# A dense layer with mish: the first two tiles of x as two loads, and the opening taken tile by tile

## The chip, the core and the metric

The kernel runs on one core of a Trainium2 chip. The metric is device time in microseconds (us) of one execution. A profile of one execution shows every engine: TensorE (PE, with its weight loads as PEld), VectorE (DVE), ScalarE (ACT), GpSimd (POOL), and SyncE (SP), which here only issues DMAs. ACT issues some DMAs too.

## The reference

```
B, S, D, F = 1, 2048, 512, 1792          # all bf16
h   = einsum("bsd,df->bsf", x, w1) + b1
sp  = log1p(exp(-abs(h))) + max(h, 0)    # softplus
act = h * tanh(sp)                       # mish
out = einsum("bsf,fd->bsd", act, w2)
```

## The kernel before

Rows of x are split into 16 tiles of 128 and, for the first product, into four blocks of 512 rows (`BLOCKS`). D is split into four parts of 128, called k, and F into 14 parts of 128, called f. The first product puts h transposed into PSUM: for each f and block, four matmuls over k, with a 128x128 piece of w1 as the stationary operand and 512 columns of the transposed x (`xT`) as the moving one. ACT reads the finished bank, adds b1 and applies mish (line 163). The second product takes a 128-row piece of that as the stationary operand and 512 columns of w2, 14 matmuls for a tile of the output; DVE copies the bank out (line 208) and SP stores it. TensorE's order is written out by hand: first product of a block, its four output tiles, the next block.

Only the opening, block 0, is unlike this. Its x tiles 2 and 3 come transposed by a DMA (`t_x23`), but tiles 0 and 1 are loaded as they are into `x_nat` by one DMA, in which partition p holds rows 2p and 2p + 1, so that "tile" j is every second row; `rows` (line 191) stores the output in the same way. TensorE transposes them against an identity matrix, half a tile at a time, in `transpose_x` (line 136), in four groups: tile 0's k 0, tile 1's k 0, k 1 of both, k 2 and k 3 of both. Each group has two PSUM banks, and DVE or ACT copies it to `xT` (line 155). `free[bank]` keeps who must be done before a bank is written again.

While these loads run, TensorE does seven filler matmuls on constants into bank 7 (`WARM`, line 105). `t_fill[n]` says that filler n is done. SP issues x, then k 1 of w1 for the first eight f (`OPEN`); it waits for the third filler, then issues the transposing load of x tiles 2 and 3, k 3, b1, the rest of w1, w2 and the other blocks of x. ACT issues k 0 and k 2 of w1 for the first eight f, at once. `load_part` (line 96) makes one such load and notes for each (k, f) which semaphore says that it has landed. SP's and ACT's loads go over two DMA queues, q1 and q10.

The opening's products are in `first` (line 239), called for a range of f, some of the four tiles and some k: k 0 of tile 0 for f 0 to 3, k 0 of tile 1 for f 0 to 3 (128 columns each), k 0 of both for f 4 to 7, k 1 and k 2 of both for f 0 to 7 (256 columns), k 0 to 2 of tiles 2 and 3 (256 columns), and k 3 of all four (512 columns), which ends each f and lets mish start. f uses bank f % 8. In `mm1_step` (line 168) TensorE waits, ahead of a product, for the bank (at the first product into it), for the piece of w1, and for the copy of x.

Of the kernel before, what the change touches and what calls it, by code (L numbers as in the profile page):

```python
# [4 lines left out]

P = 128
SQ = 32
WARM = (512,) * 5 + (256,) * 2
BLOCKS = (512, 512, 512, 512)


# [21 lines left out]
def bass_standalone__dense_activation_mish__prompt_kernel(  # L33
# [16 lines left out]
    x2, out2 = x[0], out[0]  # L50
# [3 lines left out]
    OPEN = 8  # L54
    N0 = BLOCKS[0] // P

    with ExitStack() as es:
        def sb(name, shape, t):
            return es.enter_context(nc.sbuf_tensor(name, shape, t))

        x_nat = sb("x_nat", [P, 2, D], BF)
        xT = sb("xT", [P, KT, S], BF)
# [6 lines left out]
        ident = sb("ident", [P, P], BF)  # L69
        a_sb = sb("a_sb", [P, FT, S], BF)  # L70
        o_sb = sb("o_sb", [P, S // P, D], BF)
        ps = es.enter_context(nc.psum_tensor("ps", [P, 8, 512], F32))

        def sem(name):
            return es.enter_context(nc.semaphore(name))

        sp = Stream(nc.sync, None)
        pe = Stream(nc.tensor, sem("c_pe"))
        dve = Stream(nc.vector, sem("c_dve"))
        act = Stream(nc.scalar, sem("c_act"))  # L80
        pool = Stream(nc.gpsimd, sem("c_pool"))

        def load(q, dst, src, name, transpose=False):
            s = sem(name)
            (q.eng.dma_start_transpose if transpose else q.eng.dma_start)(dst, src).then_inc(s, 16)
            return (s, 16)

        def load_w1(q, ks, a, b):
            return load(q, w1_sb[:, ks, a * P:b * P], w1v[:, ks, a * P:b * P], "s_w1_%d_%d" % (ks.start, a))
# [6 lines left out]
        def load_part(q, k0, k1, a, b):  # L96
            t = load_w1(q, slice(k0, k1), a, b)
            for f in range(a, b):
                for k in range(k0, k1):
                    t_w1[k, f] = t  # L100

        t_bz = dve.mark(nc.vector.memset(b1_nat[:, :], 0.0))  # L102
        c_w = nc.const_aps.tensor(1.0, [P, P], BF)
        c_m = nc.const_aps.tensor(1.0, [P, 512], BF)
        t_fill = [pe.mark(nc.tensor.matmul(ps[:, 7, 0:n], c_w, c_m[:, 0:n], start=True, stop=True)) for n in WARM]  # L105

        act.eng.preload_act_table(ACT.Mish)  # L107
        act.wait(t_bz)
        for k in (0, 2):
            load_part(act, k, k + 1, 0, OPEN)  # L110
        t_xn = load(sp, x_nat[:, :, :], x2[0:2 * P, :].rearrange("(p j) d -> p j d", p=P), "s_xn")
        load_part(sp, 1, 2, 0, OPEN)
        sp.wait(t_fill[2])
        t_x23 = load(sp, xT[:, :, 2 * P:4 * P], x2[2 * P:4 * P, :], "s_x23", True)
        load_part(sp, 3, 4, 0, OPEN)
# [3 lines left out]
        t = load(sp, w2_sb[:, :, :], w2v, "s_w2")  # L119
# [3 lines left out]
        for s in range(1, len(BLOCKS)):  # L123
            lo, hi = starts[s], starts[s + 1]
# [5 lines left out]
        t_id = dve.mark(nc.vector.tensor_scalar(ident[:, :], diff[:, :], 0, None, ALU.is_equal))  # L130

        free = [[] for _ in range(8)]
        t_cp = {(j, k): t_x23 for j in (2, 3) for k in range(KT)}
        t_mish = {}

        def transpose_x():

            pe.wait(t_xn, t_id)
            H = P // 2
            for b0, eng, js, ks in ((0, dve, (0,), (0,)), (2, act, (1,), (0,)), (4, dve, (0, 1), (1,)), (6, act, (0, 1), (2, 3))):  # L140
                m = len(js)
                for i, k in enumerate(ks):
                    for n, j in enumerate(js):
                        lo = (i * m + n) * H
                        for h in (0, 1):
                            g = slice(h * H, (h + 1) * H)
                            mm = nc.tensor.matmul(ps[:, b0 + h, lo:lo + H], x_nat[g, j, k * P:(k + 1) * P], ident[g, g],  # L147
                                                  start=True, stop=True)
                eng.wait(pe.mark(mm))
                for i, k in enumerate(ks):  # L150
                    dst = xT[:, k, js[0] * P:(js[-1] + 1) * P].rearrange("p (j h t) -> p j h t", j=m, h=2)
                    src = ps[:, b0:b0 + 2, i * m * H:(i + 1) * m * H].rearrange("p h (j t) -> p j h t", j=m)
                    if m == 1:
                        dst, src = dst[:, 0], src[:, 0]
                    t = eng.mark(nc.vector.tensor_copy(dst, src) if eng is dve else act.eng.activation(dst, src, ACT.Copy))  # L155
                    for j in js:
                        t_cp[j, k] = t
                free[b0] = free[b0 + 1] = [t]

        def mish(s, f, bank, t_mm):  # L160
            n = BLOCKS[s]
            act.wait(t_b1c, t_mm)
            t = act.mark(act.eng.activation(a_sb[:, f, starts[s]:starts[s + 1]], ps[:, bank, 0:n], ACT.Mish,  # L163
                                            bias=b1_sb[:, f:f + 1]))
            t_mish[s, f] = t
            free[bank] = [t]

        def mm1_step(s, f, k, bank, js=None):

            n = BLOCKS[s]  # L170
            lo, hi = (0, n) if js is None else (js[0] * P, (js[-1] + 1) * P)
            first = k == 0 and lo == 0
            if first:
                pe.wait(*free[bank])
            pe.wait(t_w1[k, f])
            if s:
                pe.wait(t_xT[s])
            else:
                pe.wait(*[t_cp[j, k] for j in (js or range(N0))])
            return nc.tensor.matmul(ps[:, bank, lo:hi], w1_sb[:, k, f * P:(f + 1) * P],  # L180
                                    xT[:, k, starts[s] + lo:starts[s] + hi], start=first, stop=(k == KT - 1 and hi == n))
# [8 lines left out]

        def rows(i):

            if i < 2:
                return out2[0:2 * P, :].rearrange("(p j) d -> p j d", p=P)[:, i, :]
            return out2[i * P:(i + 1) * P, :]

        def mm2_step(i, f, lo, hi, bank):
# [7 lines left out]
        def put(i, lo, hi, bank, t_mm, q=sp):  # L205
            nonlocal n_out
            dve.wait(t_mm)
            t = dve.mark(nc.vector.tensor_copy(o_sb[:, i, lo:hi], ps[:, bank, 0:hi - lo]))  # L208
            free[bank] = [t]
            q.wait(t)  # L210
            q.eng.dma_start(rows(i)[:, lo:hi], o_sb[:, i, lo:hi]).then_inc(s_out, 16)
            n_out += 1
# [8 lines left out]
        def mm2_last(i):  # L221

            nonlocal n_out
            cuts = (0, D - 3 * P // 2, D - P // 2, D)
            toks = []
            for n, eng in enumerate((dve, dve, act)):
                lo, hi, bank = cuts[n], cuts[n + 1], 4 + (i + n) % 4
                for f in range(FT):
                    mm = mm2_step(i, f, lo, hi, bank)
                eng.wait(pe.mark(mm))  # L230
                dst, src = o_sb[:, i, lo:hi], ps[:, bank, 0:hi - lo]
                t = eng.mark(nc.vector.tensor_copy(dst, src) if eng is dve else act.eng.activation(dst, src, ACT.Copy))  # L232
                toks.append((lo, hi, t))
            for q, (lo, hi, t) in zip((sp, sp, act), toks):
                q.wait(t)
                q.eng.dma_start(rows(i)[:, lo:hi], o_sb[:, i, lo:hi]).then_inc(s_out, 16)
                n_out += 1

        def first(fs, js, ks, last=False):
            for k in ks:  # L240
                for f in fs:
                    mm = mm1_step(0, f, k, f % 8, js)
                    if last and k == KT - 1:
                        mish(0, f, f % 8, pe.mark(mm))


        def spread_b1():
            dve.wait(t_b1)
            for j in range(P // SQ):
                t = dve.mark(nc.vector.transpose(b1_T[j * SQ:(j + 1) * SQ, :], b1_nat[:, j * SQ:(j + 1) * SQ]))  # L250
            dve.wait(t)
            return dve.mark(nc.vector.tensor_copy(b1_sb[:, :], b1_T[:, 0:FT]))  # L252

        transpose_x()
        t_b1c = spread_b1()
        first(range(4), (0,), (0,))
        first(range(4), (1,), (0,))
        first(range(4, OPEN), (0, 1), (0,))
        first(range(OPEN), (0, 1), (1, 2))
        first(range(OPEN), (2, 3), (0, 1, 2))  # L260
        first(range(OPEN), None, (3,), True)
        for f in range(OPEN, FT):
# [41 lines left out]
```

## Time and profile before

| | |
|---|---|
| device time, three runs | 104.59, 105.42, 107.27 us (median 105.42) |
| span of the profiled execution | 102.9 us |
| device time of the profiled execution itself | not given; the median lies 2.5 us above the span |
| TensorE busy | 100.2 us, 97% of the span |
| DVE, ACT busy | 13.1 us, 39.5 us |
| fillers (line 105) | 7, from 0.77 us |
| transposes (line 147) | 16, from 3.43 us |
| first product | 4.13 us |

The span runs from the first to the last instruction; the device time has the start and end of the execution around it. Busy shares are averages. For a change in the first microseconds, the rows to read are the chain of work that ended last, the timeline of the opening, and the DMA issues with their times to landing. The chain follows the last instruction back to whatever released it. In a row of the timeline stand start, duration, engine, line, operation and output<-input; "x2" says that two instructions are merged.

### The profile page before, as it was taken

What the parts mean: (1) busy time and instruction counts of PE and PEld (TensorE: products, weight loads), DVE (VectorE), ACT (ScalarE), POOL (GpSimd) and SP (SyncE); (2) the same over time, 40 slices, a digit from 0 to 9 for tenths busy, and PEclk for the clock granted to TensorE, in tenths of its full rate; (3) what the DMA queues carried; (4) which work ended last, traced back from release to release, by engine and by line L of the source; (5) the groups of instructions that cost most, each with busy time, mean ns of one, the idle gap of its engine ahead of it and who ended that gap; (6) DMA issues with size and microseconds to landing.
All of it is one profiled execution on the core that took longest, in us unless ns stands there. A gap on an engine that the chain in (4) does not pass through costs nothing.

```text
span 102.9 us, 1196 instructions
## 1 busy us (share of the span) xinstructions
PE 100.2 (97%) x527; PEld 48.8 (47%) x527; DVE 13.1 (13%) x26; ACT 39.5 (38%) x61; POOL 0.4 (0%) x5
## 2 busy tenths in 40 slices
PE   6999999999999999999999999999999999999993
PEld 2697444444444444444444444444444444444472
DVE  1203000220220000022220000022201000020241
ACT  4301999000047777000017777400006777700000
POOL 1000000000000000000000000000000000000000
DMA  2999999991110000011001000001111000001112
GB/s 61 375 283 358 363 243 112 269 237 51 51 51 0 0 6 0 0 51 51 20 31 51 0 0 10 0 3 48 51 51 51 0 0 0 0 6 51 51 51 51
DMA packets 12977, 7.94 MB, mean 77 GB/s; under 512 B 7980, under 2 KB 12332, under 8 KB 12972
## 3 DMA queue, kind: packets, MB, share of 16 engines
q1 hardware_dynamic: 12540, 7.33, 27.4%
q10 hardware_dynamic: 432, 0.54, 1.5%
q8 instruction: 4, 0.07, 0.3%
q14 instruction: 1, 0.01, 0.0%
HBM read 3.94 MB, written 2.10 MB: 59 GB/s over the span
## 4 chain that ended last, share of the span: by engine, by line
PE 97%; DVE 0%; ACT 0%; issue 0%
PE ps L180 47%; PE ps L202 47%; PE ps L105 3%; DVE xT L155 0%; ACT o_sb L232 0%; PE ps L147 0%
## 5 line engine op out<-in xcount | busy, mean ns | idle before, releaser
L163 ACT ACTIVATE a_sb<-ps,b_sb 128x512 bf16<-128x512 f32 x56 | 37.1, 698 | 47.9 <-PE ps L180 47.9
L180 PE MATMUL ps<-xT,w_sb 128*128 128x512 bf16 (+2 forms) x252 | 49.1, 355 | 0.2 <-DVE xT L155 0.2
L202 PE MATMUL ps<-w_sb,a_sb 128*128 128x512 bf16 (+3 forms) x252 | 49.1, 355 | 0.0
L180 PEld LDWEIGHTS ps<-xT,w_sb 128*128 128x128 bf16 x252 | 24.2, 98 | 24.1 <-DVE xT L155 0.3
L202 PEld LDWEIGHTS ps<-w_sb,a_sb 128*128 128x128 bf16 x252 | 23.2, 98 | 25.5
L208 DVE CAST o_sb<-ps 128x512 bf16<-128x512 f32 x15 | 10.4, 692 | 79.8 <-PE ps L202 79.8
L232 ACT ACTIVATE o_sb<-ps 128x64 bf16<-128x64 f32 x1 | 0.2, 224 | 11.5 <-PE ps L202 11.5
L105 PE MATMUL ps<-const-bfloat16-1.0 128*128 128x512 bf16 (+1 forms) x7 | 2.7, 566 | 0.8 <-PEq L289 0.8
L105 PEld LDWEIGHTS ps<-const-bfloat16-1.0 128*128 128x128 bf16 x7 | 0.9, 138 | 2.1 <-issue 2.1
L155 ACT ACTIVATE xT<-ps 128x256 bf16<-128x256 f32 (+1 forms) x3 | 0.9, 347 | 1.7 <-PE ps L147 1.7
L107 ACT ACT_TABLE_LOAD x1 | 1.3, 1283 | 0.7 <-PEq L289 0.7
L250 DVE STREAM_TRANSPOSE b_T<-b_nat 32x32 bf16<-32x32 bf16 x4 | 0.8, 202 | 3.3 <-DMA b_nat<-in_b_dram 3.2
L232 DVE CAST o_sb<-ps 128x320 bf16<-128x320 f32 (+1 forms) x2 | 0.8, 392 | 1.5 <-PE ps L202 1.5
L155 DVE CAST xT<-ps 128x128 bf16<-128x128 f32 (+1 forms) x2 | 0.6, 354 | 2.4 <-PE ps L147 2.4
L147 PEld LDWEIGHTS ps<-ident,x_nat 64*128 64x128 bf16 x16 | 0.4, 118 | 0.4 <-DMA x_nat<-in_x_dram 0.4
L147 PE MATMUL ps<-ident,x_nat 64*128 64x64 bf16 x16 | 0.5, 222 | 0.0
L130 DVE TENSOR_SCALAR ident<-diff 128x128 bf16<-128x128 int32 x1 | 0.2, 227 | 0.2 <-POOL diff L128 0.2
L128 POOL IOTA diff<- 128x128 int32 x1 | 0.2, 234 | 0.4 <-POOLq L289 0.4
L102 DVE MEMSET b_nat<- 32x64 uint32 x1 | 0.1, 112 | 0.8 <-PEq L289 0.8
L252 DVE CAST b_sb<-b_T 128x14 f32<-128x14 bf16 x1 | 0.2, 176 | 0.0
L289 POOL MEMSET const-bfloat16-1.0<- 128x1 bf16 x1 | 0.1, 102 | 0.0
L289 POOL MEMSET const-uint8-127<- 128x1 uint8 x1 | 0.1, 102 | 0.0
(2 smaller groups left out, 0.2 us busy)
## 6 DMA issues: line engine op xcount, KB each, us to landing
out_dram<-o_sb SPq DMA_DIRECT2D x15, 128.0 KB, 1.7
w_sb<-in_w_dram SPq DMA_DIRECT2D x1, 1792.0 KB, 10.7
w_sb<-in_w_dram SPq DMA_DIRECT2D x1, 768.0 KB, 6.1
w_sb<-in_w_dram ACTq DMA_DIRECT2D x2, 256.0 KB, 3.7
w_sb<-in_w_dram SPq DMA_DIRECT2D x2, 256.0 KB, 3.7
x_nat<-in_x_dram SPq DMA_DIRECT2D x1, 256.0 KB, 2.6
out_dram<-o_sb SPq DMA_DIRECT2D x1, 80.0 KB, 1.6
xT<-in_x_dram SPq DMA_TRANSPOSE x4, 5.0
```

The source lines that it names most:

```text
L105: t_fill = [pe.mark(nc.tensor.matmul(ps[:, 7, 0:n], c_w, c_m[:, 0:n], start=True, stop=True)) for n in WARM]
L107: act.eng.preload_act_table(ACT.Mish)
L128: t_diff = pool.mark(pool.eng.iota(diff[:, :], pattern=[[1, P]], base=0, channel_multiplier=-1))
L130: t_id = dve.mark(nc.vector.tensor_scalar(ident[:, :], diff[:, :], 0, None, ALU.is_equal))
L147: mm = nc.tensor.matmul(ps[:, b0 + h, lo:lo + H], x_nat[g, j, k * P:(k + 1) * P], ident[g, g], start=True, stop=True)
L155: t = eng.mark(nc.vector.tensor_copy(dst, src) if eng is dve else act.eng.activation(dst, src, ACT.Copy))
L163: t = act.mark(act.eng.activation(a_sb[:, f, starts[s]:starts[s + 1]], ps[:, bank, 0:n], ACT.Mish, bias=b1_sb[:, f:f + 1]))
L180: return nc.tensor.matmul(ps[:, bank, lo:hi], w1_sb[:, k, f * P:(f + 1) * P], xT[:, k, starts[s] + lo:starts[s] + hi], start=first, stop=( ...
L202: return nc.tensor.matmul(ps[:, bank, 0:hi - lo], a_sb[:, f, i * P:(i + 1) * P], w2_sb[:, f, lo:hi], start=(f == 0), stop=(f == FT - 1))
L208: t = dve.mark(nc.vector.tensor_copy(o_sb[:, i, lo:hi], ps[:, bank, 0:hi - lo]))
L232: t = eng.mark(nc.vector.tensor_copy(dst, src) if eng is dve else act.eng.activation(dst, src, ACT.Copy))
L250: t = dve.mark(nc.vector.transpose(b1_T[j * SQ:(j + 1) * SQ, :], b1_nat[:, j * SQ:(j + 1) * SQ]))
```

## The change

x tiles 0 and 1 are loaded by two DMAs, each of 128 consecutive rows, and the output of these tiles is stored in consecutive rows too. There are six fillers instead of seven. ACT waits for the second filler before it issues anything, and then issues k 0 of w1 as two loads (f 0 to 3, f 4 to 7; `HALF` is 4) and k 2. The transposes are done tile by tile: for each tile DVE copies k 0 and ACT copies k 1, 2 and 3 together, 128x384. The products then take k 0 of tile 0, k 0 of tile 1 and k 1 of both for f 0 to 3, k 0 and k 1 of both for f 4 to 7, and k 2 of both for f 0 to 7; the rest is as before.

```diff
--- before.py
+++ after.py
@@ -5,7 +5,8 @@
 
 P = 128
 SQ = 32
-WARM = (512,) * 5 + (256,) * 2
+WARM = (512,) * 5 + (256,)
+HALF = 4
 BLOCKS = (512, 512, 512, 512)
 
 
@@ -105,11 +106,12 @@
         t_fill = [pe.mark(nc.tensor.matmul(ps[:, 7, 0:n], c_w, c_m[:, 0:n], start=True, stop=True)) for n in WARM]
 
         act.eng.preload_act_table(ACT.Mish)
-        act.wait(t_bz)
-        for k in (0, 2):
-            load_part(act, k, k + 1, 0, OPEN)
-        t_xn = load(sp, x_nat[:, :, :], x2[0:2 * P, :].rearrange("(p j) d -> p j d", p=P), "s_xn")
+        t_xn = [load(sp, x_nat[:, i, :], x2[i * P:(i + 1) * P, :], "s_xn%d" % i) for i in range(2)]
         load_part(sp, 1, 2, 0, OPEN)
+        act.wait(t_fill[1])
+        load_part(act, 0, 1, 0, HALF)
+        load_part(act, 0, 1, HALF, OPEN)
+        load_part(act, 2, 3, 0, OPEN)
         sp.wait(t_fill[2])
         t_x23 = load(sp, xT[:, :, 2 * P:4 * P], x2[2 * P:4 * P, :], "s_x23", True)
         load_part(sp, 3, 4, 0, OPEN)
@@ -135,27 +137,26 @@
 
         def transpose_x():
 
-            pe.wait(t_xn, t_id)
             H = P // 2
-            for b0, eng, js, ks in ((0, dve, (0,), (0,)), (2, act, (1,), (0,)), (4, dve, (0, 1), (1,)), (6, act, (0, 1), (2, 3))):
-                m = len(js)
-                for i, k in enumerate(ks):
-                    for n, j in enumerate(js):
-                        lo = (i * m + n) * H
+            pe.wait(t_id)
+            for i in (0, 1):
+                pe.wait(t_xn[i])
+                for eng, b0, ks in ((dve, 2 * i, (0,)), (act, 4 + 2 * i, (1, 2, 3))):
+                    m = len(ks)
+                    for n, k in enumerate(ks):
                         for h in (0, 1):
                             g = slice(h * H, (h + 1) * H)
-                            mm = nc.tensor.matmul(ps[:, b0 + h, lo:lo + H], x_nat[g, j, k * P:(k + 1) * P], ident[g, g],
-                                                  start=True, stop=True)
-                eng.wait(pe.mark(mm))
-                for i, k in enumerate(ks):
-                    dst = xT[:, k, js[0] * P:(js[-1] + 1) * P].rearrange("p (j h t) -> p j h t", j=m, h=2)
-                    src = ps[:, b0:b0 + 2, i * m * H:(i + 1) * m * H].rearrange("p h (j t) -> p j h t", j=m)
+                            mm = nc.tensor.matmul(ps[:, b0 + h, n * H:(n + 1) * H], x_nat[g, i, k * P:(k + 1) * P],
+                                                  ident[g, g], start=True, stop=True)
+                    eng.wait(pe.mark(mm))
+                    dst = xT[:, ks[0]:ks[-1] + 1, i * P:(i + 1) * P].rearrange("p k (h t) -> p k h t", h=2)
+                    src = ps[:, b0:b0 + 2, 0:m * H].rearrange("p h (k t) -> p k h t", k=m)
                     if m == 1:
                         dst, src = dst[:, 0], src[:, 0]
                     t = eng.mark(nc.vector.tensor_copy(dst, src) if eng is dve else act.eng.activation(dst, src, ACT.Copy))
-                    for j in js:
-                        t_cp[j, k] = t
-                free[b0] = free[b0 + 1] = [t]
+                    for k in ks:
+                        t_cp[i, k] = t
+                    free[b0] = free[b0 + 1] = [t]
 
         def mish(s, f, bank, t_mm):
             n = BLOCKS[s]
@@ -190,8 +191,6 @@
 
         def rows(i):
 
-            if i < 2:
-                return out2[0:2 * P, :].rearrange("(p j) d -> p j d", p=P)[:, i, :]
             return out2[i * P:(i + 1) * P, :]
 
         def mm2_step(i, f, lo, hi, bank):
@@ -253,10 +252,11 @@
 
         transpose_x()
         t_b1c = spread_b1()
-        first(range(4), (0,), (0,))
-        first(range(4), (1,), (0,))
-        first(range(4, OPEN), (0, 1), (0,))
-        first(range(OPEN), (0, 1), (1, 2))
+        first(range(HALF), (0,), (0,))
+        first(range(HALF), (1,), (0,))
+        first(range(HALF), (0, 1), (1,))
+        first(range(HALF, OPEN), (0, 1), (0, 1))
+        first(range(OPEN), (0, 1), (2,))
         first(range(OPEN), (2, 3), (0, 1, 2))
         first(range(OPEN), None, (3,), True)
         for f in range(OPEN, FT):
```

## The prediction

> **What bounds the kernel now.** I read the page's totals first, then the chain of work that ended last in order of time.
>
> ```profile
> span 102.9 us, 1196 instructions
> ...
> PE 100.2 (97%) x527; PEld 48.8 (47%) x527; DVE 13.1 (13%) x26; ACT 39.5 (38%) x61; POOL 0.4 (0%) x5
> ```
> ```profile
> 0.77 2.72 PE ps L105 x7
> 3.49 0.19 PE ps L147 x3
> ...
> 3.70 0.30 DVE xT L155
> 4.00 0.12 issue
> 4.13 12.32 PE ps L180 x84
> 16.45 12.09 PE ps L202 x56
> ```
>
> TensorE is busy for 97% of the span, and from 4.13 us on nothing else is in the chain until the very end. The second and later stages are 56 matmuls of 512 columns in 12.09 us, 0.216 us each, so 256 columns take 0.108 and 128 columns 0.054. The change touches no product after the opening. So it can be worth only what it does to the time at which TensorE gets through the opening, and all of that lies in the first 4.13 us and in the waits that an earlier or later start meets behind them. The profiled execution has a span of 102.9 us; its own device time is not given. The median of the runs shown, 105.42, lies 2.5 us above the span, and I carry a difference in the span over to it one to one.
>
> Next the DMA, because the opening is fed by it: who issued what when, and how long each load took to land. The rows come from the timeline of SP and ACT and from the lists of DMA issues of short windows, where a load stands alone.
>
> ```profile
> 0.74 0.40 SPq L85 DMA_DIRECT2D x_nat<-in_x_dram  x1
> 0.95 0.86 ACTq L85 DMA_DIRECT2D w_sb<-in_w_dram  x2
> 1.19 0.42 SPq L85 DMA_DIRECT2D w_sb<-in_w_dram  x1
> 1.36 0.46 ACTq L85 DMA_DIRECT2D w_sb<-in_w_dram  x1
> 2.24 1.31 SPq L85 DMA_TRANSPOSE xT<-in_x_dram  x1
> 4.73 0.41 SPq L85 DMA_DIRECT2D w_sb<-in_w_dram  x1
> ```
> ```profile
> x_nat<-in_x_dram SPq DMA_DIRECT2D x1, 256.0 KB, 2.6
> w_sb<-in_w_dram ACTq DMA_DIRECT2D x1, 256.0 KB, 3.0
> w_sb<-in_w_dram SPq DMA_DIRECT2D x1, 256.0 KB, 3.6
> w_sb<-in_w_dram ACTq DMA_DIRECT2D x1, 256.0 KB, 4.3
> xT<-in_x_dram SPq DMA_TRANSPOSE x1, 4.4
> w_sb<-in_w_dram SPq DMA_DIRECT2D x1, 768.0 KB, 6.1
> ```
>
> Issue plus time to landing gives: x tiles 0 and 1 at 3.34, w1 k0 (first eight f) at 3.95, k1 at 4.79, k2 at 5.66, x tiles 2 and 3 at 6.64, the rest of w1 at 10.83. Against them stand the first uses, counted with the matmul times above: k1 at 4.13 + 8 x 0.054 + 4 x 0.108 = 4.99, k2 0.86 later at 5.86, x tiles 2 and 3 another 0.86 later at 6.72, the rest of w1 at 6.72 + 24 x 0.108 + 8 x 0.216 = 11.04. The slacks are 0.20, 0.20, **0.08** and 0.21 us. TensorE shows no wait, but each load arrives just ahead of its use.
>
> The last view is the DMA itself: the queues in the windows 1.78 to 2.78 and 2.78 to 3.44, then the busy share and rate by stretch (the last two columns).
>
> ```profile
> q1 hardware_dynamic: 116, 0.24, 94.6%
> ...
> q10 hardware_dynamic: 116, 0.24, 96.3%
> q1 hardware_dynamic: 26, 0.02, 9.3%
> ```
> ```profile
> 2.80:3.40 0.60, 0.60 (x3) 0.15 (x1) 0.00 (x0) 0.00 (x0) 0.00 (x0) 1.00 1.05 389
> 3.40:4.10 0.70, 0.56 (x17) 0.42 (x17) 0.40 (x2) 0.34 (x2) 0.00 (x0) 1.00 1.05 389
> 4.10:4.80 0.70, 0.67 (x11) 0.66 (x12) 0.23 (x1) 0.56 (x2) 0.00 (x0) 1.00 1.02 379
> ```
>
> q1 is SP's queue, q10 ACT's. The DMA engines are full, and they serve the loads **one after another**: in the first window only x moves, in the second almost only w1 k0, though k1 was issued on the other queue at 1.19. At 389 GB/s a load of 256 KB takes 0.67 us, half of one 0.34. So the landings of k1, k2 and x tiles 2 and 3 are set by the bytes ahead of them.
>
> **The change part by part.** *The filler.* One 256-column filler less. The first two rows below are weight loads, each made as a filler begins: the fifth at 2.43, the sixth at 2.86, one pitch of 512 columns (0.43 us) later. The sixth, of 256, streams for 0.21, so TensorE is free at 3.07 instead of 3.28, worth 0.21 if x is there.
>
> ```profile
> 2.43 0.15 PEld L105 LDWEIGHTS ps<-const-bfloat16-1.0 128*128 128x128 bf16 x1 [0.28 <-issue]
> 2.86 0.15 PEld L105 LDWEIGHTS ps<-const-bfloat16-1.0 128*128 128x128 bf16 x1 [0.28 <-issue]
> ...
> 3.42 0.42 PEld L147 LDWEIGHTS ps<-ident,x_nat 64*128 64x128 bf16 x16 [0.41 <-DMA x_nat<-in_x_dram]
> ```
> ```profile
> out_dram<-o_sb SPq DMA_DIRECT2D x15, 128.0 KB, 1.7
> ```
>
> *x as two loads.* The transposes now start at 3.42, 0.08 after x landed. No row shows a 128 KB load at this place; the 128 KB stores land 1.7 us after issue, so tile 0 lands between 2.44 and 3.34. I take 2.9, the middle, which leaves the filler's end, 3.07, as the start. Tile 1 finishes with the same 256 KB moved and lands at 3.34 as now. It costs SP one more issue, 0.45 us (0.74 to 1.19), so w1 k1 leaves SP at 1.64 instead of 1.19. The transpose load behind it waits for the third filler until 2.24 anyway, and k1 is off the queue by 2.06, so nothing later on SP moves. The stores of rows 0 to 255 only change their addresses.
>
> *Transposes and copies.* Still 16 transposes, now eight behind each tile. Copies by shape:
>
> ```profile
> L155 ACT ACTIVATE xT<-ps 128x256 bf16<-128x256 f32 x2 | 0.7, 381 | 0.0
> ...
> L155 DVE CAST xT<-ps 128x256 bf16<-128x256 f32 x1 | 0.4, 415 | 0.0
> L155 DVE CAST xT<-ps 128x128 bf16<-128x128 f32 x1 | 0.3, 292 | 2.4 <-PE ps L147 2.4
> ...
> L155 ACT ACTIVATE xT<-ps 128x128 bf16<-128x128 f32 x1 | 0.3, 278 | 1.7 <-PE ps L147 1.7
> ```
> ```profile
> L163 ACT ACTIVATE a_sb<-ps,b_sb 128x512 bf16<-128x512 f32 x56 | 37.1, 698 | 47.9 <-PE ps L180 47.9
> ```
>
> DVE gets two copies of 128x128 (2 x 0.292 for 0.292 + 0.415 now). ACT gets two of 128x384, a shape not in the trace: between 0.381 and 0.698, and 0.278 + 2 x 0.103 = 0.48 by the step from 128 to 256 columns, which I take. Now, transposes to first copy's end is 3.42 to 4.00, 0.58; so tile 0's k 0 is ready at 3.65 and tile 1's at 4.00. ACT starts tile 0 at about 3.50 (0.43 for the four transposes' pairs and their drain, 3.07 on) and ends it at 3.98, and ends tile 1 at 4.46. That copy carries k 1, so no k 1 product starts before about 4.50. And f 2 and 3 use the PSUM banks of tile 1's DVE copy: they wait until 4.0.
>
> *w1 k 0 behind the second filler, as two loads.* SP's transpose load leaves at 2.24 behind filler 3, so ACT's first half leaves one pitch earlier, at 1.81, instead of 0.95. Queued behind this wait on ACT are the second half (2.2) and k 2 (2.7 instead of 1.36), and the copies at 3.5, which are not delayed. Now k0 is second in the row of loads; behind the change x tile 0, x tile 1 and **k1 (1.64) have all been issued before it**. If loads are served in the order of issue, as all those of this trace were, the first half follows k1: 3.34 + 0.67 + 0.34 = 4.35. With the 0.08 from landing to TensorE the first product starts at 4.43 instead of 4.13. Bounds: if the half goes ahead of k1, 3.34 + 0.34 = 3.68, and the copies gate instead; if k1 takes the 0.84 that lay between the landings of k0 and k1 (3.95, 4.79) and the half as much as half of that, 4.60, a start at 4.68.
>
> The Trainium skill has a rule that speaks against the order of issue. In "DMA: Bandwidth & Descriptors", section "Queues, rings and completion order", it says that each DMA engine takes turns between the queues that have work, a packet at a time. By that rule the half would follow x tile 1, and k1 come third; the trace cannot decide, since its four loads alternate SP, ACT, SP, ACT.
>
> *The sum.* Start 4.43; j 0 and j 1 of f 0 to 3 take 8 x 0.054 (4.86); k1's copies are there (4.50), and the same 20 products of 256 columns as now lead up to x tiles 2 and 3 at 4.86 + 2.16 = 7.02, against 6.72 now. Those landed at 6.64; even the slip of some bytes stays covered, as do the rest of w1 (11.34 against 10.83) and k2 (6.16 against 5.66, with 0.5 to spare). So the slip of 0.30 goes through to the end: 105.42 + 0.30 = **105.7**. The filler's 0.21 and tile 0's earlier landing are not seen, since the weights are late. Forecast's own range by the bounds above: 105.6 to 106.0.
>
> **Rivals.** *The half of k0 goes ahead of k1 (not slower).* Then f 0 and 1 start at about 3.75, f 2 and 3 at 4.1, the 128-column products end at 4.43, k1 waits for ACT's copy to 4.50, and x tiles 2 and 3 are wanted at 6.66. They land at 6.64 and are usable at 6.72, where they are used now. Start 0.38 earlier, gain 0.00 to 0.06: 105.36 to 105.42. Even with x tiles 2 and 3 early, the rest of w1 allows no more than its slack of 0.21, 105.2. For it: the separate queue; against it: k1 is issued 0.17 earlier.
>
> *k2 falls behind x tiles 2 and 3.* k2 is now issued at 2.7, the transpose load at 2.24, as before. If the order turns, k2 lands where the transpose load did, 6.64, usable at 6.72, 0.86 later than now; if they share, half of it. Every product behind it slips: 105.42 + 0.43 to 0.86, about 106.1. It decides as soon as k2 lands past its first use, 5.8 to 6.2. Against it: the transpose load's issue takes 1.31 us, to 3.55, so its work may come late enough.
>
> *TensorE's clock.* Fillers come 0.43 apart for 512 columns, products 0.216: between 3.07 and 4.13 TensorE doubled its speed, 2.3 to 3.4 us after the first filler, though the page shows a granted clock of 1.00 throughout. With less filler and a hole from about 3.6 to 4.43, the step might need as long again from 4.43, at half speed: half of 2.3 to 3.4, 1.2 to 1.7 slower, 106.6 to 107.1. The fillers and transposes still cover nearly the same stretch, which speaks against it. "TensorE: Matmul & The Clock Gate" of the Trainium skill, Part 1, puts the step at a free-running window's end, whatever the kernel; by that, the phase would differ from run to run, before and after alike.
>
> **How the numbers follow.** Forecast 0.50, not slower 0.28, k2 late 0.15, clock 0.05, anything else 0.02. The cases run from 105.2 to 106.3, the clock aside. The three runs shown lie between 104.59 and 107.27, so a median of such runs can itself move by some tenths, and I widen by 0.6 below and 0.4 above: 104.6 to 106.7. Two per cent, about what a measurement of this kernel can tell from no change, is 2.1 us; only a clock that stays low through a run comes near it. Faster 0.01, within 0.95, slower 0.04.
>
> **What would show it.** In the profile after: the transposes from about 3.07 and in two groups; k0's first half landing near 4.35 with k1 ahead of it in the DMA windows; the first product at about 4.43 with a wait for w1 named ahead of it; the rest of the opening 0.3 later. A first product near 3.75 and a hole before k1 means the first rival, a wait ahead of k2's products the second, products 0.43 apart per 512 columns past 4.5 the third. I am wrong if the half lands before 3.8, or if x tiles 2 and 3 land so much earlier that an early start lasts.

## The result: 108.0 us, slower by 2.9%

The changed kernel takes 108.03 us (median of six runs, 107.64 to 111.77); the kernel before, run beside it, 105.12 (104.59 to 107.27). The ratio is 1.0294, 95% interval [1.0248, 1.0340]. The forecast was 105.7, its range 104.6 to 106.7. Ratios here and below leave out runs that lie over 1.5% above the fastest of their own kernel; for three kernels below (k2_on_sp, x23_plain, alternate) that is half of the runs or more, so for those the median of all runs stands beside the ratio.

The profiled execution of after has a span of 107.5 us, 4.6 more than before's. That is more than the 2.9 between the medians: in every run on record the device time lies 1.3 to 1.4 us above the span, so before's profiled execution (span 102.9) took about 104.2, as little as the fastest of its runs, while after's took 108.86, 0.8 above its median. Of the 2.5 us that the prediction saw between before's span and median, 1.2 are this, and its slacks are those of an execution in which things went well. What follows accounts for the 4.6 of this pair.

The page's totals, then the chain of work that ended last (start, duration, what):

```profile
span 107.5 us, 1187 instructions
...
PE 101.4 (94%) x517; PEld 49.5 (46%) x526; DVE 13.0 (12%) x26; ACT 39.5 (37%) x60; POOL 0.4 (0%) x5
```
```profile
2.23 0.46 ACTq L86
...
2.72 7.76 DMA w_sb<-in_w_dram
...
10.53 3.67 PE ps L181 x32
...
21.10 3.88 PE ps L201 x18
```

TensorE is busy for 101.4 us instead of 100.2, and idle for 6 instead of 3. In before nothing but TensorE's work stood in the chain from 4.13 us on. Here one load of w1, k 2, issued by ACT at 2.72, holds the end until 10.48. The second product of block 0 starts at 21.10 instead of 16.45: the 4.65 us are all lost before that, and nothing is added behind.

Who issued what and when, in SP's and ACT's timeline (start, duration, instruction, count):

```profile
0.74 0.87 SPq L86 DMA_DIRECT2D x_nat<-in_x_dram  x2
1.66 0.42 SPq L86 DMA_DIRECT2D w_sb<-in_w_dram  x1
2.25 1.31 SPq L86 DMA_TRANSPOSE xT<-in_x_dram  x1
...
1.82 1.35 ACTq L86 DMA_DIRECT2D w_sb<-in_w_dram  x3
```

And how long each took to land, from the lists of DMA issues of short windows around each issue (KB, us from issue to landing), in the order of issue: x tile 0, x tile 1, k 1, the two halves of k 0, x tiles 2 and 3, k 2.

```profile
x_nat<-in_x_dram SPq DMA_DIRECT2D x1, 128.0 KB, 2.1
x_nat<-in_x_dram SPq DMA_DIRECT2D x1, 128.0 KB, 2.0
w_sb<-in_w_dram SPq DMA_DIRECT2D x1, 256.0 KB, 3.7
w_sb<-in_w_dram ACTq DMA_DIRECT2D x1, 128.0 KB, 3.7
w_sb<-in_w_dram ACTq DMA_DIRECT2D x1, 128.0 KB, 4.3
xT<-in_x_dram SPq DMA_TRANSPOSE x1, 8.5
w_sb<-in_w_dram ACTq DMA_DIRECT2D x1, 256.0 KB, 7.8
```

x lands early, at 2.8 and 3.2. Then k 1 lands at 5.4 (before: 4.79), the halves of k 0 at 5.5 and 6.5 (k 0 before: 3.95), k 2 at 10.5 (before: 5.66) and x tiles 2 and 3 at 10.7 (before: 6.64). The bytes are the same. By stretch (last two columns: DMA busy share, GB/s), first after, then before:

```profile
5.40:6.40 1.00, 0.74 (x8) 0.77 (x9) 0.00 (x0) 0.00 (x0) 0.00 (x0) 1.00 1.23 94
6.40:7.40 1.00, 1.00 (x8) 0.73 (x7) 0.00 (x0) 0.00 (x0) 0.00 (x0) 1.00 1.15 128
...
8.40:9.60 1.20, 0.83 (x4) 0.28 (x2) 0.00 (x0) 0.00 (x0) 0.00 (x0) 1.00 0.99 152
```
```profile
5.40:6.40 1.00, 1.00 (x11) 0.90 (x10) 0.00 (x0) 0.00 (x0) 0.00 (x0) 1.00 1.19 296
6.40:7.40 1.00, 1.00 (x11) 0.90 (x10) 0.00 (x0) 0.00 (x0) 0.00 (x0) 1.00 1.05 269
...
8.40:9.60 1.20, 1.20 (x13) 0.98 (x11) 0.18 (x2) 0.00 (x0) 0.00 (x0) 1.00 1.01 361
```

Between 5.4 and 9.6 us the DMA engines count as fully busy, 0.99 to 1.23, in both kernels, but after moves 94 to 152 GB/s and before 269 to 361. So packets are under way and do not get done. The queues in the microsecond from 5.4, after and then before (packets, MB, share):

```profile
q10 hardware_dynamic: 21, 0.04, 68.4%
q1 hardware_dynamic: 199, 0.05, 54.8%
```
```profile
q1 hardware_dynamic: 605, 0.30, 118.5%
```

In before ACT's queue (q10) is empty by then and SP's moves alone. In after both are at work, ACT's 21 packets, pieces of w1, take more of the engines' time than SP's 199, and together they move a third of the bytes.

TensorE's own timeline in after (start, duration, instruction, count, and in brackets the idle time ahead of it with what ended it) shows a second loss. In the rows above the granted clock, the column ahead of the DMA's, is 1.00 throughout; the durations say otherwise.

```profile
3.21 0.61 PE L149 MATMUL ps<-ident,x_nat 64*128 64x64 bf16 x16
5.66 3.57 PE L181 MATMUL ps<-xT,w_sb 128*128 128x128 bf16 x20 [1.84 <-DMA w_sb<-in_w_dram]
10.53 0.72 PE L181 MATMUL ps<-xT,w_sb 128*128 128x256 bf16 x5 [1.29 <-DMA w_sb<-in_w_dram]
```
```profile
L181 PE MATMUL ps<-xT,w_sb 128*128 128x256 bf16 x12 | 2.8, 418 | 0.0
```
```profile
L180 PE MATMUL ps<-xT,w_sb 128*128 128x256 bf16 x44 | 5.0, 273 | 0.0
```

The second and third of these fences are groups of matmuls by shape (busy us, mean ns of one): after from 5.6 to 9.1 us, before from 4.1 to 9.4. The first 20 products take 3.57 us; at before's pace they are 8 x 0.054 + 12 x 0.108 = 1.73. One of 256 columns lasts 418 ns instead of 273: TensorE runs at half its pace, until about 9. Then it waits 1.29 for k 2, and from 10.53 its pace is full. In this execution k 2 covers the slow pace; with k 2 in time it would have shown.

So along TensorE's timeline the opening loses 1.53 at the first product (5.66 against 4.13), 1.84 by the pace (3.57 against 1.73) and 1.29 waiting for k 2, 4.66 together. But k 2 alone would have cost as much here: its products start at 10.53, and at 5.86 in before, by the prediction's count.

### The profile page after: what moved, and what is told of

Read it like the earlier page. It is cut to its first block, busy times and chain, and to the rows that moved or that the text cites. A ratio compares the mean times of both kernels' runs of the same rounds, so it can differ in the third digit from the quotient of the medians.

```text
span 107.5 us, 1187 instructions
## 1 busy us (share of the span) xinstructions
PE 101.4 (94%) x517; PEld 49.5 (46%) x526; DVE 13.0 (12%) x26; ACT 39.5 (37%) x60; POOL 0.4 (0%) x5
## 4 chain that ended last, share of the span: by engine, by line
PE 88%; DMA 7%; ACT 1%; ACTq 1%; issue 1%
PE ps L201 45%; PE ps L181 43%; DMA w_sb<-in_w_dram 7%; ACT L108 1%; ACTq L86 1%; ACT o_sb L231 0%
## 5 line engine op out<-in xcount | busy, mean ns | idle before, releaser
L181 PE MATMUL ps<-xT,w_sb 128*128 128x512 bf16 (+2 forms) x247 | 50.5, 365 | 3.4 <-DMA w_sb<-in_w_dram 3.1
L181 PEld LDWEIGHTS ps<-xT,w_sb 128*128 128x128 bf16 x252 | 25.1, 101 | 28.1 <-issue 2.0
L156 ACT ACTIVATE xT<-ps 128x384 bf16<-128x384 f32 x2 | 0.9, 488 | 1.6 <-PE ps L149 1.6
L156 DVE CAST xT<-ps 128x128 bf16<-128x128 f32 x2 | 0.5, 292 | 2.2 <-PE ps L149 2.2
```

## Experiments

**First theory: the loads no longer go one at a time.** ACT's wait puts k 0 and k 2 on the second queue while SP's k 1 and transposing load run. Rivals: k 2 is simply late; the transposing load's issue holds up others. Four kernels, ratios to before (104.44 us):

```diff
 no_wait (after):        -act.wait(t_fill[1])
 k2_on_sp (after):       k2's load_part moved from act to sp, behind k1
 before_late_k2 (before): load_part(act, 0, ...); +act.wait(t_fill[3]); load_part(act, 2, ...)
 before_wait (before):   -act.wait(t_bz)  +act.wait(t_fill[1])
```

no_wait: 

> The changed kernel without ACT's wait for the second filler: k 0's halves leave at about 0.95 and 1.4, k 2 at 1.8, ahead of the transposing load at 2.24. Three theories. Overlap theory (k 2 on ACT's queue is in flight together with the transposing load on SP's, and both crawl: 94 to 152 GB/s between 5.4 and 9.6 us, against 311 to 389 before): k 2 is mostly through before the transposing load's packets come, lands by 6, time 104.7 to 105.8. Late-start theory (k 0's first half lands at 5.53 behind k 1, TensorE has a hole and runs its first 20 products at half pace; all of the loss would follow from that): the half lands by 3.8, first product by 4.1, the same time. Order theory (transposes, copies and products tile by tile cost the time): stays at 107 or more.

k2_on_sp: 

> The changed kernel with only k 2 moved: SP issues it right behind k 1, ahead of its wait, so k 2 and the transposing load are in one queue and can't share the engines; k 0's halves still wait and go over ACT's queue. Overlap theory: no crawl, 300 GB/s or more from 5.4 us on, k 2 lands by 7 instead of 10.48; the first product stays near 5.5 and the first 20 products at half pace to about 9.0, so TensorE goes on 1.5 us earlier than in the changed kernel: 106.3 to 106.9. Late-start theory with nothing from k 2: no better than 107.5, since the start is unchanged. Order theory: 107.5 or more.

before_late_k2: 

> The kernel before with one edit: ACT waits for the fourth filler ahead of k 2, which leaves at 2.7 instead of 1.36, as in the changed kernel; k 0, x, transposes and order as before. First product stays at 4.13 at full pace. Overlap theory: k 2 meets the transposing load, both crawl, k 2 lands at 8 to 10, time 107.5 to 109.5. Late-start and order theory: k 2 lands one load later at most, 6.6, time 105.1 to 106.1.

before_wait: 

> The kernel before with one edit: ACT waits for the second filler ahead of k 0 and k 2 (one load each), which leave at 1.8 and 2.25; x in one load, order as before. Late-start theory: k 0 lands behind k 1, about 4.8 to 5.5, first product about 5 to 5.6; k 2 leaves beside the transposing load (2.25), so the overlap theory expects a crawl as well and k 2 at 8 to 10: both expect 107 to 109. Order theory: 105.1 to 105.6, with the first product after 4.13 by no more than 0.4.

Measured: no_wait 108.92 us, ratio 1.0408 [1.0352, 1.0464]. k2_on_sp 107.31, ratio 1.0120 [1.0065, 1.0174]. before_late_k2 106.25, 1.0168 [1.0127, 1.0209]. before_wait 109.38, 1.0424 [1.0337, 1.0510]. Not all of this was expected: no_wait lies far above the 104.7 to 105.8 of both theories of the loads, before_late_k2 between its two ranges, before_wait just above its own. The chain of no_wait, then of before_late_k2:

```profile
1.66 5.66 DMA w_sb<-in_w_dram
7.36 13.18 PE ps L180 x76
```
```profile
2.67 5.62 DMA w_sb<-in_w_dram
8.34 10.57 PE ps L181 x64
```

k2_on_sp gives back part of the loss at its best and little of it in the median. no_wait is the surprise. With the wait gone and both halves of k 0 issued ahead of k 1, the time is *worse*: now k 1 is the late one, 5.66 us from issue. So the wait isn't the only cause, and being late isn't a property of ACT's loads. In before, ACT's wait alone, which holds k 0 to 1.82 and k 2 behind it, costs 4.2%, and k 2 alone, held to 2.67, 1.7%. The chain of before_wait, then its matmuls by shape from 6.7 to 11.6 and from 11.7 to 14.3 us:

```profile
1.82 4.82 DMA w_sb<-in_w_dram
6.78 14.70 PE ps L180 x84
```
```profile
L180 PE MATMUL ps<-xT,w_sb 128*128 128x256 bf16 x19 | 4.3, 417 | 0.0
...
L180 PE MATMUL ps<-xT,w_sb 128*128 128x256 bf16 x25 | 3.0, 280 | 0.0
```

This run shows the slow pace by itself. TensorE starts 2.65 us later than before (6.78 against 4.13), waits for nothing after that, and yet needs 14.70 us for the 84 products that took 12.32: 2.38 more. 2.65 + 2.38 = 5.03; the spans differ by 5.0 (107.9 against 102.9). The products are at half pace until about 11.7, 4.9 us after the restart, and at full pace from then on.

**Is it the transposing load, the two queues, or the first access to w1?** Ratios to before at 104.61 us, touch to 104.67:

```diff
 x23_plain (after):        the transposing load of x tiles 2, 3 made a plain one of the same bytes
 x23_after_k2 (after):     -sp.wait(t_fill[2])  +sp.wait(t_fill[2], t_w1[2, 0])
 one_queue (after):        no ACT loads; SP: x 0, x 1, both halves of k0, k1, k2
 no_wait_x23_late (no_wait): sp.wait(t_fill[2]) -> sp.wait(t_fill[4])
 touch (after):            + load(act, w_t, w1v[:, :, 0:32], ...) ahead of ACT's wait
```

x23_plain leaves out the transposition of x tiles 2 and 3.

x23_plain: 

> The changed kernel with x tiles 2 and 3 loaded by a plain load of the same bytes to the same place instead of a transposing one (the transposition of these two tiles is left out). Issue theory, new after the first four runs: packets are slow (200 to 1400 ns instead of 84) in just those loads that are issued from about 0.6 us ahead of the transposing load's issue (2.24) until its end; k 1 at 1.66 and k 0 and k 2 at 1.8 to 2.7 fall into that stretch, in the kernel before nothing does. It expects no slow packets of w1 here, 300 GB/s or more from 2.6 us on, k 2 landed by 6, time 104.4 to 105.6. Two-queue theory (a queue of SP and one of ACT that are busy together slow each other, whatever they carry): 2.6 to 3.4 us stays near 149 GB/s, k 2 lands after 6.5, time 106 or more.

x23_after_k2: 

> The changed kernel in which SP waits for k 2's landing ahead of the transposing load, so that this load's issue and transfer meet no load of ACT's. Issue theory: k 1, k 0 and k 2 run at 300 GB/s or more, k 2 lands by 5.8; the transposing load is issued only then and lands at 8 to 8.6, TensorE waits for it about 1.3 us: 105.6 to 106.6. Two-queue theory: k 1 and k 0 stay slow from 2.6 to 4.4 as in the changed kernel, k 2 lands at 6 to 7 and the transposing load at 9 or later: 106.6 to 108.

one_queue: 

> The changed kernel with k 0's halves, k 1 and k 2 all issued by SP in this order behind x; ACT issues no load, and the transposing load follows k 2 directly, at about 3.4. Issue theory: k 0 and k 1 are issued before the stretch and are fast, the half lands near 3.7; k 2, issued at 3.0, is inside it and slow, landing at 6 to 7: 104.8 to 106.0. Two-queue theory: nothing is slow, k 2 lands by 5.6: 104.1 to 104.8.

no_wait_x23_late: 

> The changed kernel without ACT's wait, and with the transposing load behind the fifth filler instead of the third, so that it is issued at about 3.1 instead of 2.24, 1 us behind the last of k 1 and k 2 (1.66 and 1.67 to 2.1). Issue theory: no load is in the stretch, k 1 and k 2 are fast, k 2 lands by 5.6, x tiles 2 and 3 by 6.8: 104.1 to 105.0. Two-queue theory: k 1 and k 2, both in flight from 3.2 us on two queues, crawl as without the wait alone (k 2 landed at 7.5 there, 108.9 us): 107 or more.

touch: 

> The changed kernel with one more load: ACT, ahead of its wait, loads the first 64 bytes of each of the 512 rows of w1 into a tile that nothing reads. After eight runs the issue theory and the two-queue theory are both out (k 1 stalls with a plain load in the transposing load's place, and with all loads on one queue). What is common: the first packets of a load issued at about 1.66 us or later take 300 to 1400 ns. First-access theory: these rows of w1 were not read before, and the first read of a region is slow; in the kernel before this is hidden because all four loads are issued by 1.36 us. It expects no packets of k 1 above 300 ns here, first product by 4.5, 105 to 106.5. Queue theory (the stall comes from a short queue: a load is slow unless about 1 us of work lies ahead of it in the engines): k 1 is as slow as in the changed kernel, 107.5 to 109.

Measured: x23_plain 107.73 us, ratio 1.0191 [1.0107, 1.0275]. x23_after_k2 108.06, 1.0315 [1.0254, 1.0377]. one_queue 106.77, 1.0158 [1.0069, 1.0246]. no_wait_x23_late 108.69 (106.30 to 109.18; too scattered for a ratio). touch 107.95, 1.0264 [1.0193, 1.0336]. None comes back to before. Without a transposing load k 2 lands sooner in the profiled execution (108.54 us), 8.0 instead of 10.5, but k 0's half still at 5.5: the transposing load may make it worse and isn't the start of it. In x23_after_k2 k 2 lands at 6.2, and then x tiles 2 and 3 are the late ones, 9.8. With every one of these loads on SP's queue (profiled execution: 107.48 us) k 1 still lands at 6.1, 3.5 after its issue: two queues don't seem to be needed. And a piece of each row of w1 read beforehand changes nothing. The queue theory in touch's expectation, that a load is slow unless about 1 us of work lies ahead of it, doesn't fit no_wait: there k 1 had x and all of k 0 ahead of it, 512 KB, 1.3 us at the 389 GB/s of before (an estimate), and still took 5.66.

**Which part of the change does it?** Each part alone, in before (104.67 us):

```diff
 x_split_only (before):    the two loads of x, consecutive rows
 k0_split_only (before):   k0 as two loads
 tile_order_only (after):  before's loads and seven fillers; transposes, copies, products of after
```

x_split_only: 

> The kernel before with x tiles 0 and 1 as two loads of consecutive rows, nothing else; k 1 moves from 1.19 to 1.66 on SP, k 0 and k 2 stay at 0.95 and 1.36 on ACT. Queue and first-access theory: k 1, issued at 1.66, is reached with little ahead of it and stalls, lands at 5.3 to 6.5 instead of 4.79, and is wanted at 4.99: 105.3 to 107. If it is not the time of issue that matters: 104.2 to 104.9.

k0_split_only: 

> The kernel before with k 0 as two loads, nothing else; k 2 moves from 1.36 to about 1.8 on ACT. x, k 0 and k 1 lie ahead of k 2, so by the queue theory it has over 1 us of work ahead of it and is fast: 104.2 to 105. If every load issued after about 1.6 us stalls: k 2 lands at 6 to 7.5 instead of 5.66 and is wanted at 5.86, 105 to 106.5.

tile_order_only: 

> The changed kernel's transposes, copies and product order with all loads and fillers as in the kernel before (x in one load, k 0, k 1 and k 2 at 0.95, 1.19 and 1.36). Theories of the loads: all loads land as in the kernel before, first product within 0.2 us of 4.13, 104.2 to 104.9. Order theory: 106 or more.

Measured: x_split_only 107.20 us, ratio **1.0239** [1.0184, 1.0294]; k0_split_only 104.80, 1.0013 [0.9980, 1.0045]; tile_order_only 104.75, 1.0021 [0.9991, 1.0050]. The tile order is free and worth nothing, and so is k 0's split. x as two loads costs nearly what the whole change costs. TensorE in x_split_only:

```profile
4.28 0.61 PE L147 MATMUL ps<-ident,x_nat 64*128 64x64 bf16 x16 [0.79 <-issue]
4.91 1.89 PE L180 MATMUL ps<-xT,w_sb 128*128 128x128 bf16 x12
7.31 1.98 PE L180 MATMUL ps<-xT,w_sb 128*128 128x256 bf16 x9 [0.51 <-DMA w_sb<-in_w_dram]
```

The same three losses: tile 1 of x lands at 4.2 and the first product comes 0.78 later; the first 12 products take 1.89 instead of 0.86; then a wait for k 1 until 7.31, issued at 1.66, 5.6 to landing.

**Why does x as two loads cost?** It delays k 1 (1.19 to 1.66, behind k 2 at 1.36), halves the pieces to 1 KB, and adds a load. Ratios to before at 105.02 us (the first three) and 104.55:

```diff
 k1_late (before):   + sp.wait(t_fill[1]) ahead of k1            (k1 at 1.82, x one load)
 turns (before):     x split; + act.wait(t_fill[1]) ahead of k2   (k1 1.66, k2 1.82: in turn)
 alternate (after):  sp: x 0, k0, k2; act: x 1, k1; all early, no wait
 x_1kb (before):     x one load, "(j p) d -> p j d": 1 KB pieces
 x_halves (before):  x two loads of 64 partitions, 2 KB pieces
 k2_at_182 (before): + act.wait(t_fill[1]) ahead of k2            (turns without the split)
```

k1_late: 

> Before, with one change: SP waits for the second filler ahead of w1 k1, which so leaves at about 1.82 us instead of 1.19, behind k0 (0.95) and k2 (1.36), which both come from ACT. x stays one load. If the split of x costs by its own smaller pieces, k1 lands by about 5.6 us and the time is that of before, within 1%. If what costs is that k1 comes out of its turn (k0 and k2 behind one another on ACT's queue, k1 beside them from SP's), k1 lands past 6.5 us, the first k1 products wait for it, and the ratio is 1.015 to 1.03, as for the kernel with x split alone (1.024).

turns: 

> Before with x tiles 0 and 1 as two loads (k1 so leaves SP at about 1.66 us), and ACT waits for the second filler ahead of w1 k2, which so leaves at about 1.82 instead of 1.36: the w1 loads go in turn again, k0 from ACT, k1 from SP, k2 from ACT, only later than before. If the turn matters, k1 lands near 5.0 us, k2 near 5.8, and the ratio is 0.99 to 1.005. If it matters that a load is issued by about 1.4 us, k1 or k2 lands past 6.5 us and the ratio is 1.015 to 1.04. If the 1 KB pieces of the split x matter, the same.

alternate: 

> After's tile order, six fillers and consecutive rows, but no wait on ACT and every load whole and early, in turn between the queues: SP x tile 0 (0.74 us), ACT x tile 1 (about 0.8), SP w1 k0 (about 1.2), ACT k1 (about 1.25), SP k2 (about 1.65), then x tiles 2 and 3 as before. If early and in turn is what keeps the loads whole, k0 lands by 3.8, k1 by 4.7, k2 by 5.6, the first product comes by 4.1 and the ratio is 0.995 to 1.003. If two loads beside one another on two queues stall each other whatever their order, k1 or k2 lands past 6 us and the ratio is above 1.01.

x_1kb: 

> Before, with x tiles 0 and 1 still one load, issued at 0.74 us, but of consecutive rows: each piece of it is 1 KB instead of 2 KB, and twice as many. k1 leaves at 1.19 as before. If the smaller pieces of x are what upsets the loads behind it, k1 or k2 lands past 6.5 us and the ratio is 1.015 to 1.03. If two loads in place of one do it, nothing changes: 0.997 to 1.004.

x_halves: 

> Before, with x tiles 0 and 1 as two loads of 64 partitions each, whose pieces stay 2 KB; k1 leaves SP at about 1.66 us. If a second load for x (its issue, and k1 behind it) is what upsets the others, the ratio is 1.015 to 1.03 with k1 or k2 past 6.5 us. If the 1 KB pieces do it, 0.997 to 1.005.

k2_at_182: 

> Before, with one wait: ACT waits for the second filler ahead of w1 k2, which leaves at about 1.82 us instead of 1.36; x is one load, k1 leaves at 1.19. It differs from the kernel turns in the split of x alone. If the split is what cost there, k2 lands by 5.9 us and the ratio is 0.997 to 1.005; if it was k2 on ACT's queue issued close to the transposing load on SP's, k2 lands past 6.3 us and the ratio is 1.01 to 1.02, part of the 1.017 measured with k2 at 2.68.

Measured: k1_late 105.22 us, ratio 1.0030 [1.0002, 1.0058]. turns 107.01, 1.0209 [1.0157, 1.0260]. alternate 106.64 (104.83 to 108.59), ratio of its best runs 1.0033 [0.9984, 1.0082]. x_1kb 104.51, **0.9989** [0.9948, 1.0031]. x_halves 108.13, **1.0298** [1.0225, 1.0371]. k2_at_182 105.30, 1.0037 [0.9998, 1.0075].

The pair x_1kb and x_halves decides: small pieces in one load cost nothing, large pieces in two loads cost 3%. k1_late rules out that k 1's delay, or its place behind k 2, does it by itself. turns and k2_at_182 differ in the split (and in the 0.47 by which it delays k 1, which k1_late clears): 2.1% against 0.4%. The theory that keeping the loads in turn between the queues is what counts falls with turns. The chains of x_halves, x_1kb, k1_late and turns:

```profile
0.74 3.02 DMA x_nat<-in_x_dram
3.77 3.05 issue
...
7.45 6.63 PE ps L181 x52
```
```profile
4.32 5.42 PE ps L180 x52
```
```profile
4.35 13.24 PE ps L181 x84
```
```profile
1.66 5.25 DMA w_sb<-in_w_dram
6.96 12.05 PE ps L181 x72
```

and, in x_halves, the DMA issue of the second half of x, the microsecond from 5.4, and SP's queue in it:

```profile
x_nat<-in_x_dram SPq DMA_DIRECT2D x1, 128.0 KB, 5.4
```
```profile
5.40:6.40 1.00, 0.00 (x0) 0.00 (x0) 0.00 (x0) 0.00 (x0) 0.00 (x0) 1.00 2.69 176
```
```profile
q1 hardware_dynamic: 476, 0.17, 265.2%
```

In x_halves the late load is x itself: its second half, issued at 1.37, ahead of k 1 and the transposing load, lands 5.4 later, the 3.05 us of "issue" being that wait. TensorE starts at 7.45, 3.32 later than before, and its first 52 products take 6.63 against x_1kb's 5.42, 1.21 of slow pace; 3.32 + 1.21 = 4.53, and the spans differ by 4.5 (107.4 against 102.9). The DMA engines' busy share is 2.69 at 176 GB/s, nearly all of it SP's: several packets of one queue lie open on an engine at once, and wait. k1_late, in which TensorE waits for no load, also has a trace of slow pace, 13.24 against 12.32 for 84 products, in a run as fast as before's usual ones.

The chain of alternate:

```profile
5.30 12.43 PE ps L179 x84
```

In this execution (105.48 us) its products start at 5.30, late, but at nearly the full pace, 12.43 against 12.32. All its runs spread over 3.8 us where 23 runs of before beside it spread over 1.3 (104.24 to 105.55), and its median is 1.5% over theirs: with x split, loads early and in turn come through sometimes, not reliably. No kernel of the 18 beat the kernel before.

## Why the prediction was wrong

**What bounds the kernel: right.** All of the loss lies in the opening, and every microsecond of it goes to the end.

**The step that failed: "they serve the loads one after another", in the order of issue, at 0.67 us each.** From it came the first half of k 0 at 4.35, with 4.60 as the late bound; it landed at 5.5, and the first product started at 5.66 instead of 4.43. The order held here, k 1 landing just ahead of the half; that each load gets the engines' full rate until it is done did not. The step was read from one execution, a fortunate one, in which the loads hardly overlapped, and made into a rule for loads side by side. x_halves and x_split_only show that even x in two pieces ends it, with k 0 and k 2 issued about where they were and k 1 0.5 to 0.8 later. The rival, the half ahead of k 1 at 3.68 and no loss, was as wrong. The Trainium skill's rule beside it ("DMA: Bandwidth & Descriptors", section "Queues, rings and completion order"), that the engines take turns between the queues, agrees with the queue rows as far as they go (q10 and q1 both at work from 5.4 to 6.4); taking turns alone doesn't explain 94 GB/s.

**The second failing step: k 2 "with 0.5 to spare".** It landed at 10.5, 4.3 after 6.16, and in the profiled execution that alone fixes the end. The sum kept k 2's old landing, 5.66, though k 2 leaves at 2.7 instead of 1.36; by the order of issue, the rule used for k 0, it belonged behind x tiles 2 and 3, issued at 2.24. The rival "k2 falls behind x tiles 2 and 3" (0.15) named the wait that ended up last in the chain, and mis-sized it: its 0.43 to 0.86 took the landing of x tiles 2 and 3, 6.64, as fixed, and they landed at 10.7.

**TensorE's clock (0.05): about right in size, too low in chance.** The forecast's sum had this term at nothing. The rival's condition, less filler and a hole ahead of the first product, was met, and beside its price of 1.2 to 1.7 the runs show 1.21 in x_halves, 2.38 in before_wait and 1.84 in after, there covered by the wait for k 2. But that condition isn't what decides. before_late_k2 has all seven fillers and its first product at 4.26, and its first 20 products take 3.09 us instead of 1.73, by the row below; alternate has six fillers, starts at 5.30 and loses only 0.11. What sets the slow pace off isn't shown.

```profile
4.26 3.09 PE L181 MATMUL ps<-xT,w_sb 128*128 128x128 bf16 x20 [0.23 <-DMA w_sb<-in_w_dram]
```

That "only a clock that stays low through a run comes near" 2% was false. The Trainium skill ("TensorE: Matmul & The Clock Gate", Part 1) gives full speed after about 3.4 us of sustained work, in a window that runs freely. The 4.9 us of before_wait from restart to full pace is longer; work that starts just inside one window would need nearly two, 6.8 us (an estimate from that page), so the trace agrees in kind, as does a loss that differs between such runs with a window that runs freely.

**What held.** The transposes start at 3.21 (said: 3.07), x tile 0 lands at 2.8 (2.9). The 128x384 copies of ACT take 488 ns (0.48 was taken), by the row below, from 3 to 5.4 us. SP's transposing load leaves at 2.25 as said, and the filler's 0.21 was not seen.

```profile
L156 ACT ACTIVATE xT<-ps 128x384 bf16<-128x384 f32 x2 | 0.9, 488 | 1.6 <-PE ps L149 1.6
```

**What stays open.** Shown is which edits do it (x as two loads; ACT's loads of k 0 and k 2 held to 1.82 and after), that the DMA engines, though busy, then move a third to two thirds of before's bytes from 5.4 to 6.4 us, and how that becomes time. Why the packets stall isn't shown. It isn't the size of the pieces, k 1's delay alone, the number of loads as such (k0_split_only has as many as x_split_only) or the transposing load alone; as far as touch and one_queue reach, it isn't a first access to w1 or the presence of two queues either. Nor is it only that the second load of x leaves behind k 0: where it does, x itself is late (4.2 in x_split_only, 6.8 in x_halves), but in after and in one_queue both leave ahead of k 0, x lands by 3.4, and w1's loads are the late ones. The shorter filler was not tried alone. That the wait and the split together (2.9%) cost less than the wait alone (4.2%, the intervals just touch) is also without an explanation.

## What to carry to other kernels

A set of loads that lands back to back in one profile says nothing of what they do when one more is put among them or one is issued 0.5 us later: price a late load with the slowest landing that a neighbouring edit can cause, here 2 to 5 us late and not 0.7, and give a real chance to it. Judge a split load by its number of loads and by its piece size separately, in kernels that change one of them. Where TensorE's first work may come late, count two things: the start, and 1 to 2.4 us for a half pace of the next few microseconds, which some of these openings had and others not.

## What the runs showed of the hardware that I had not expected

Busy DMA engines can move little: 1.23 busy at 94 GB/s in after, 2.69 at 176 in x_halves, against 1.19 at 296 in before. In the lists shown, a load of 128 KB took from 2.0 to 5.4 us to land, one of 256 KB from 2.6 to 7.8. And TensorE's pace can stay at half for 4.9 us of dense products (417 ns for one of 256 columns, later 280) with a granted clock of 1.00 in every row of the profile.
